# A SiLU MLP's first product: three of eight feature pairs by 11 block products instead of 12, in five half chunks

## The chip, the core and the metric

The kernel runs on one core of one Trainium2 chip. The core has a matrix engine (PE, with its weight loads shown as PEld), a vector engine (DVE), a scalar engine (ACT), a general engine (POOL), a queue that issues transfers (SP) and 16 DMA engines. Each engine executes its own instructions in the order in which the program issued them; they meet at semaphores. The metric is device time in microseconds.

## What is computed

A delta-rule recurrence over 768 tokens of 4 batches and 8 heads, then an MLP with SiLU. The MLP is what the change is about: `x` is 3072 x 384, `w_in` 384 x 2048, `w_out` 2048 x 384.

```python
def _attn_ref(q, k, v, beta):            # B, H, S, D = 4, 8, 768, 48
    k_n = k / (np.linalg.norm(k, axis=-1, keepdims=True) + 1e-06)
    for t in range(S):
        y[:, :, t] = np.einsum('bhd,bhde->bhe', q[:, :, t], state)
        v_old = np.einsum('bhde,bhd->bhe', state, kt)
        state = state + bt[:, :, :, None] * np.einsum('bhd,bhe->bhde', kt, vt - v_old)

def _moe_ref(x, w_in, w_out):
    h = x @ w_in
    g = h * (1.0 / (1.0 + np.exp(-h)))
    return (g @ w_out).astype(np.float32)
```

The weights come as 64-bit floats and are narrowed to f32 on the chip; all products are f32.

## The kernel before

The sequence is cut into six chunks of 128 tokens, each chunk into two halves of 64. For a half chunk, `solve(c)` advances the recurrence and leaves `xTs[c, hf]`: the MLP's input, transposed, as three blocks of 128 input features by 256 columns (4 batches x 64 tokens). `hidden(c, hf)` (line 1022) makes the first product and its SiLU; `combine(c, hf)` (line 1122) makes the second product in a Strassen form on 192-column matmuls (line 1136; chunk 0 has a plain second product, `project`). `feed_forward` is one after the other.

`hidden` runs over eight feature pairs `f`. A pair is two blocks of 128 output features, each the sum of three matmuls (128x128 weights from `w_in`, 256 columns from `xTs`), so six matmul calls that fill one PSUM bank of 512 columns; one ACT instruction then writes SiLU of all 512 columns to a `gT` tile (line 1039). An f32 matmul call is two instructions in the trace. The banks of room `M`, `m0` and `m1`, alternate from pair to pair (`bank`, line 61). Three pairs share a `gT` tile; there are three such tiles, the last with one slot of 512 columns unused. Every second or third pair DVE adds the sums that `combine` needs (`sum_g`, line 1110).

The order of the work is the order of the program text: `pin` (line 78) ties every instruction to the one before it on its engine. The stages are Python generators; `go` and `run` advance them by a step, and a `yield` is where other work can come in between. In the main loop (lines 1499 to 1527) the nine steps of `solve(c)`, then `prepare(c + 1)` (scores of the next chunk) and `invert(c + 1)` (31 rank-one updates on DVE) are interleaved with the steps of the MLP. `hidden(c, 0)` for chunks 2 to 5 falls beside the end of `solve(c)`, where ACT makes two bursts of seven copies (`even_heads`, line 915: six to `xT` and one to `part`), and beside `prepare(c + 1)`: DVE transposes from `stage` (`turn_blocks`, line 471), scores (`score`, line 504) that ACT copies out and DVE masks (`mask`, line 526; `by_act` and `by_dve`, lines 531 and 534). `hidden(c, 1)` falls beside `invert`. The last half, chunk 5's second, runs with nothing beside it.

The keys of chunk `c` lie in `kbufs[c % 2]`, in rows of 64 of which 48 are used; `square` (line 361), `turn` (line 481) and `update` (line 841) read them. `stage` holds chunk 1's turned keys and queries, and from chunk 2 on, in its first three quarters, the blocks that `load_blocks` brings in (line 149).

Of the kernel before, what the change touches and what calls it, by code (L numbers as in the profile page):

```python
# [10 lines left out]
FP32 = mybir.dt.float32  # L11
U32 = mybir.dt.uint32
ACTF = mybir.ActivationFunctionType
ALU = mybir.AluOpType
# [5 lines left out]
def kernel(  # L20
# [10 lines left out]
    nc = tc.nc  # L31
    B, H, S, D = q.shape
    DM, DFF = moe_w_in.shape
    P = 128
    C = P
    assert S % C == 0 and D == 48 and H == 8 and B == 4 and DM == H * D and DM == 3 * P
    NCH = S // C
    NP = H // 2
    BH = B * H
    W = 64  # L40
    T = 32
    NB = C // T
    NKT = DM // P
    NFF = DFF // P
    HB = B // 2
    HH = HB * H
    GT = B * W
    FG = 3
# [7 lines left out]
    mlp = ctx.enter_context(tc.tile_pool(name="mlp", bufs=2))  # L56
    banks = ctx.enter_context(tc.tile_pool(name="banks", bufs=1, space=PSUM))
    A, CC, M = deque(("a0", "a1", "a2")), deque(("c0", "c1", "c2")), deque(("m0", "m1"))
    kept_banks = {tag: banks.tile([P, 512], FP32, name=f"pb_{tag}", tag=tag) for tag in CC}

    def bank(room, name):

        tag = room[0]
        room.rotate(-1)
        return kept_banks.get(tag) or banks.tile([P, 512], FP32, name=name, tag=tag)
# [3 lines left out]
    def behind(later, earlier, how=NoSync):  # L69

        tc.add_manual_dep(
            later.ins, earlier.ins.name,
            mybir.DependencyInfo(how, mybir.DependencyReason.DATA), reason="order",
        )
# [3 lines left out]
    def pin(op):  # L78

        engine = op.ins.engine  # L80
        if engine in pins:
            behind(op, pins[engine])
        pins[engine] = op
        return op
# [3 lines left out]
    def in_line(dma):  # L88

        if line:  # L90
            behind(dma, line[-1])
        if pace:
            behind(dma, pace.pop(), Sync)
        line.append(dma)
        return dma
# [8 lines left out]
    def go(steps, n=1):  # L104
        for _ in range(n):
            next(steps, None)
# [9 lines left out]

    kbufs = [const.tile([P, B, NP, 2, W], FP32, name=f"kb{s}") for s in range(2)]
    zbuf = const.tile([P, B, 2, NP, W], FP32, name="z")
    vfs = {}
    LO, HI = slice(0, W), slice(W, P)  # L120
    HALVES = (LO, HI)

    def on(e, hf, g):

        return HALVES[hf ^ e ^ g]

    sums_of_g = const.tile([P, 2, NFF // 2, C], FP32, name="sums_of_g")
# [5 lines left out]
    def load_pair(to, src, c, bs):  # L133

        for g in range(bs.start // HB, bs.stop // HB):
            us = slice(HB * g, HB * (g + 1))
            for e, hf in ((g, None), (1 - g, 0), (1 - g, 1)):
                rows = slice(0, P) if hf is None else on(e, hf, g)
                tokens = slice(c * C, (c + 1) * C) if hf is None else slice(c * C + hf * W, c * C + (hf + 1) * W)
                in_line(nc.sync.dma_start(  # L140
                    out=to[rows, us, :, e, 0:D],
                    in_=src[us, e::2, tokens, :].rearrange("b h t d -> t b h d"),
                ))

    RUN = C // T * D
    stage = const.tile([P, B * NP * 2 * C], FP32, name="stage")
# [16 lines left out]
    def in_blocks(c):  # L163

        return 1 < c < NCH
# [7 lines left out]

    def load_k(c, bs=ALL):
        if c < NCH:
            load_pair(kbufs[c % 2], k, c, bs)

    def load_q(c, bs=ALL):
        if c < NCH:
# [25 lines left out]
    for e in range(2):  # L205
        for g in range(2):
            to, of = slice(HH * e + HH // 2 * g, HH * e + HH // 2 * (g + 1)), slice(HH // 2 * g, HH // 2 * (g + 1))
# [6 lines left out]
    w_in = const.tile([P, NKT, DFF], FP32, name="w_in")  # L214
# [83 lines left out]
    def narrow_w_out(i):  # L298
# [14 lines left out]
        out=above[0:W], in_=above[0:W], pattern=[[1, W]], compare_op=ALU.is_gt, fill=0.0,  # L313
# [3 lines left out]
        out=above[W:P], in_=above[W:P], pattern=[[1, W]], compare_op=ALU.is_gt, fill=0.0,  # L317
# [5 lines left out]
    for j in range(NB):  # L323
        rows = slice(T * j, T * (j + 1))
# [36 lines left out]
    def square(c, b):  # L361

        if b == 0:
            sums[c] = small.tile([P, BH], FP32, name="ss", bufs=1)[:]
        if c > 2:
            squared[c, b] = zbuf[:, b].rearrange("p s a w -> p (s a) w")[:, :, 0:D]
        elif b % HB == 0:
            tag = "g" if c > 0 or b > 0 else "x"
            both = work.tile([P, HB, H, D], FP32, name="sq", tag=tag, bufs=1)
            for u in range(HB):  # L370
                squared[c, b + u] = both[:, u]
        kb = kbufs[c % 2][:, b].rearrange("p a e w -> p (a e) w")[:, :, 0:D]
        pin(nc.gpsimd.tensor_tensor(out=squared[c, b], in0=kb, in1=kb, op=ALU.mult))

    def add_squares(c, b):
# [155 lines left out]
    def by_act(to, of):  # L531
        return pin(nc.scalar.copy(to, of))  # L532
# [219 lines left out]
    xTs, parts = {}, {}  # L752
# [88 lines left out]
    def update(c, g, hf):  # L841

        if c == NCH - 1 and hf == 1:
            return
        pu = bank(CC, "pu")
        for u, p, e, n, of, _ in of_heads():
            rows = on(e, hf, g)
            yield pin(nc.tensor.matmul(  # L848
                pu[of, n * D : (n + 1) * D], lhsT=kbufs[c % 2][rows, g * HB + u, p, e, 0:D],
                rhs=zbuf[rows, g * HB + u, hf, p, 0:D], start=True, stop=True,  # L850
            ))
        to = states[g][:, :, :, 0:D]
        pin(nc.vector.tensor_tensor(out=to, in0=to, in1=by_heads(pu), op=ALU.add))
# [160 lines left out]
    gTs = {}  # L1014

    def hidden_of(c, hf, f):

        if (c, hf) == (0, 1):
            return turned_kq[:].rearrange("p b j a t -> p (b j a t)")[:, f * 2 * GT : (f + 1) * 2 * GT]
        return gTs[f // FG][:, f % FG, :]  # L1020

    def hidden(c, hf):

        for f in range(NFF // 2):
            assert ("in", f) in narrowed
            ph = bank(M, "phid")
            for j in range(2):
                for a in range(NKT):
                    pin(nc.tensor.matmul(  # L1029
                        ph[:, j * GT : (j + 1) * GT],  # L1030
                        lhsT=w_in[:, a, (2 * f + j) * P : (2 * f + j + 1) * P],
                        rhs=xTs[c, hf][:, a, :],
                        start=(a == 0), stop=(a == NKT - 1),
                    ))
                if j == 0:
                    yield
            if f % FG == 0 and (c, hf) != (0, 1):
                gTs[f // FG] = mlp.tile([P, FG, 2 * GT], FP32, name="gT", bufs=3)
            pin(nc.scalar.activation(  # L1039
                out=hidden_of(c, hf, f), in_=ph[:], func=ACTF.Silu, scale=-0.5 if in_blocks(c) else 0.5  # L1040
            ))
            if c > 0 and f % FG == 1 and f >= FG:
                for which in (S1, S2):
                    sum_g(which, f // FG - 1)
            yield
# [41 lines left out]
    def sum_w():  # L1087
# [14 lines left out]
    S1, S2, S3, S4 = (  # L1102
        (0, (0, 1), (1, 1), ALU.add), (1, 0, (0, 0), ALU.subtract),
        (0, (0, 0), (0, 1), ALU.subtract), (1, (1, 0), 1, ALU.subtract),
    )
# [4 lines left out]
    def sum_g(which, g):  # L1110
        k, left, right, op = which
        fs = group(g)
        of = [
            sums_of_g[:, x, fs] if isinstance(x, int) else
            gTs[g][:, 0 : fs.stop - fs.start, x[0] * GT + x[1] * C : x[0] * GT + (x[1] + 1) * C]
            for x in (left, right)
        ]
        pin(nc.vector.tensor_tensor(out=sums_of_g[:, k, fs], in0=of[0], in1=of[1], op=op))  # L1118
# [154 lines left out]
    for b in range(B):  # L1273
        square(0, b)
# [95 lines left out]
    def run(n=1):  # L1370

        for _ in range(n):
            name = next(needed, None)
            if name is not None:
                until(name)
            go(pieces)
            begin_soon()
# [121 lines left out]
    for c in range(1, NCH):  # L1499
        if c > 1:  # L1500
            solving = solve(c)
            for n in range(9):
                go(solving)
                run((2, 2, 2, 2, 1, 1, 2, 2, 2)[n])
                if n == 5:
                    pieces = chained(pieces, feed_forward(c, 0), feed_forward(c, 1))
        assert next(solving, 0) == 0
        go(long_2, 99)
        if c + 1 < NCH:
            ready = prepare(c + 1)  # L1510
            go(ready)
            run(2)
            step = block_steps(c + 1)
            for _ in ready:
                run(2)
            run(6)
            for n, _ in enumerate(invert(c + 1, step)):
                run(int(n % 4 != 3 and n != 24))
                if n == 3:
                    load_k(c + 2)  # L1520
                    if in_blocks(c + 2):
                        load_blocks(k, c + 2, ALL)
            after = lengths(c + 2) if c + 2 < NCH else iter(())
            for _ in range(8 if c == 1 else 10):
                run()
                go(after, 4)
            go(after, 99)
# [31 lines left out]
```

## Time and profile before

| what | value |
|---|---|
| runs | 653.5, 654.77, 656.47 us, median 654.77 |
| profiled execution | 652.37 us, its span 650.4 us |
| granted TensorE clock, mean | 0.99 |
| feature pairs in all | 12 half chunks x 8 |
| L1029, matmuls of `hidden` | 1152 instructions, 260.1 us busy |
| L1039, SiLU of a pair | 0.597 us each |
| `hidden` of the last half | 608.13 to 628.85 us |

The profile is of one execution. PE, PEld, DVE, ACT and POOL are given as busy time, share of the span and number of instructions. A row of a group has the line, engine, operation, output and inputs, the shape and the count; then busy us in all, mean ns of one; then the engine's idle time just before them and what ended most of it. A row of the timeline has the start in us, the length in us, the engine, the line, the operation and, in brackets, the idle time before it and what released it. The chain of waits is followed back from the last instruction, at each step to what released it or to the instruction before it on its engine. Matmul records overlap, since the engine is pipelined: a record of 0.379 us can be followed by the next after 0.216.

### The profile page before, as it was taken

The page shows a single profiled execution, that of the slowest core. Times are in us where ns is not written, and L with a number is a line of the kernel's source. Part 1 is how long each engine was busy: PE and PEld are TensorE (multiplying, and loading weights), DVE is VectorE, ACT ScalarE, POOL GpSimd, SP SyncE. Part 2 cuts the span into 40 slices and gives each one's busy share as a digit, 9 for nine tenths or more (in the row PEclk, how much of TensorE's full clock was granted, in tenths as well). Part 3 has the DMA queues.
Part 4 walks back from the last instruction along what each step waited for, and adds up shares of the span by engine and source line. Part 5 has one row for each costly group of instructions (what it writes and reads, how often), then busy time and mean ns, then how long its engine had stood idle before and what let it go on. Part 6 is the DMA issues. An engine that isn't in the chain of part 4 may idle for free.

```text
span 650.4 us, 21395 instructions
## 1 busy us (share of the span) xinstructions
PE 627.6 (96%) x9416; PEld 548.0 (84%) x9416; DVE 397.6 (61%) x911; ACT 213.8 (33%) x497; POOL 90.9 (14%) x92
## 2 busy tenths in 40 slices
PE   7878899999989999999999999999999999999997
PEld 5577778756779989989989989989989989889997
DVE  5875689997764987453986453987454974103112
ACT  2455663332342122451122452122451122451111
POOL 5023631334101020010020010020011000000000
PEclk9979999999989999999999999999999999999999
DMA  9876534250288324268324268324173024100101
GB/s 136 209 165 206 192 75 104 98 97 3 53 154 148 58 73 60 50 136 143 59 76 57 48 131 146 61 74 60 28 153 72 10 65 60 40 13 1 25 0 25
DMA packets 145676, 54.70 MB, mean 84 GB/s; under 512 B 117152, under 2 KB 138912, under 8 KB 145584
## 3 DMA queue, kind: packets, MB, share of 16 engines
q1 hardware_dynamic: 143136, 52.93, 39.6%
q8 instruction: 74, 1.21, 0.8%
q10 hardware_dynamic: 2448, 0.41, 0.4%
q14 instruction: 18, 0.15, 0.1%
HBM read 40.14 MB, written 11.01 MB: 79 GB/s over the span
## 4 chain that ended last, share of the span: by engine, by line
PE 91%; DMA 2%; issue 2%; DVE 2%; ACT 1%; SPq 1%; DVEq 0%
PE phid L1029 38%; PE px L1136 16%; PE py L1136 12%; PE po L1064 5%; PE pb_c L828 3%; PE pa L517 2%; PE pb_c L816 2%; PE pyc L907 2%; PE pb_c L1064 2%; PE pb_c L848 1%; PE pb_c L336 1%; PE pyc L894 1%; DMA kb<-in_k_dram 1%; PE pt L488 1%; PE py L770 1%
## 5 line engine op out<-in xcount | busy, mean ns | idle before, releaser
L1029 PE MATMUL phid<-xT,w_in 128*128 128x256 f32 x1152 | 260.1, 383 | 2.1 <-DMA xT<-part 2.0
L1029 PEld LDWEIGHTS phid<-xT,w_in 128*128 128x128 f32 x1152 | 216.9, 191 | 34.4 <-issue 3.0
L1039 ACT ACTIVATE gT<-phid 128x512 f32<-128x512 f32 x88 | 52.5, 597 | 149.8 <-PE phid L1029 145.2
L615 DVE SCALAR_TENSOR_TENSOR rank<-g,step,x 128x31 f32<-128x31 f32 (+15 forms) x124 | 49.8, 401 | 35.8 <-DMA g<-blocks 32.3
L1118 DVE TENSOR_TENSOR sums_of_g<-gT 128x384 f32<-128x384 f32 (+1 forms) x60 | 29.9, 518 | 59.0 <-ACT gT L1039 48.4
L1136 PE MATMUL py<-w_out,sums_of_g 128*128 128x192 f32 x320 | 56.8, 329 | 0.0
L1136 PE MATMUL px<-sums_of_w,sums_of_g 128*128 128x192 f32 x320 | 56.8, 329 | 0.0
L1136 PEld LDWEIGHTS px<-sums_of_w,sums_of_g 128*128 128x128 f32 x320 | 52.2, 190 | 0.5
L1136 PEld LDWEIGHTS py<-w_out,sums_of_g 128*128 128x128 f32 x320 | 52.2, 190 | 0.4
L620 DVE TENSOR_TENSOR x<-x,rank 128x31 f32<-128x31 f32 (+15 forms) x124 | 42.5, 343 | 4.3
L455 POOL TENSOR_TENSOR vf<-vf,n_slot 128x768 f32<-128x768 f32 x10 | 15.0, 1516 | 169.3 <-DMA vf<-in_v_dram 125.3
L476 DVE STREAM_TRANSPOSE kq<-stage 128x512 f32<-128x512 f32 x28 | 28.5, 1114 | 12.0 <-DMA stage<-in_q_dram 10.4
L532 ACT COPY xT<-pyc 48x128 f32<-48x128 f32 (+2 forms) x126 | 32.6, 259 | 1.6
L1136 PE MATMUL px<-sums_of_w,gT 128*128 128x192 f32 x160 | 28.4, 329 | 0.0
L1136 PE MATMUL py<-w_out,gT 128*128 128x192 f32 x160 | 28.4, 329 | 0.0
L1136 PE MATMUL px<-w_out,gT 128*128 128x192 f32 x160 | 28.0, 327 | 0.0
L1136 PEld LDWEIGHTS px<-w_out,gT 128*128 128x128 f32 x160 | 26.4, 190 | 0.5
L538 POOL COPY g<-x 64x256 f32<-64x256 f32 x4 | 5.0, 1241 | 154.5 <-DVE x L623 154.5
L1136 PEld LDWEIGHTS py<-w_out,gT 128*128 128x128 f32 x160 | 26.1, 190 | 0.3
L1136 PEld LDWEIGHTS px<-sums_of_w,gT 128*128 128x128 f32 x160 | 26.1, 190 | 0.2
L828 PEld LDWEIGHTS pb_c<-vf,xi 64*64 64x64 f32 x736 | 23.5, 138 | 3.2 <-issue 2.9
L1147 DVE TENSOR_TENSOR o<-o,kept 128x192 f32<-128x192 f32 (+1 forms) x29 | 11.5, 422 | 24.0 <-ACT kept L1144 24.0
(221 smaller groups left out, 921.6 us busy)
## 6 DMA issues: line engine op xcount, KB each, us to landing
vf<-in_v_dram SPq DMA_DIRECT2D x48, 96.0 KB, 3.2
out_dram<-o SPq DMA_DIRECT2D x42, 96.0 KB, 2.2
w_out<-in_moe_w_in_dram SPq DMA_DIRECT2D x4, 768.0 KB, 4.4
sums_of_w<-in_moe_w_out_dram SPq DMA_DIRECT2D x4, 768.0 KB, 5.9
blocks<-ap SPq DMA_DIRECT2D x44, 64.0 KB, 1.9
g<-blocks SPq DMA_DIRECT2D x5, 512.0 KB, 3.5
kb<-in_k_dram SPq DMA_DIRECT2D x12, 192.0 KB, 5.1
kb<-in_k_dram SPq DMA_DIRECT2D x24, 96.0 KB, 4.6
```

The costliest lines, as they stand in the source:

```text
L455: pin(nc.gpsimd.tensor_tensor(out=vf, in0=vf, in1=of, op=ALU.mult))
L476: pin(nc.vector.transpose(out=kqs[c, b][:, :, j, :].rearrange("p a (i m) -> p a m i", i=T), in_=src.rearrange("p a (m d) -> p a m d", d=D) ...
L517: pin(nc.tensor.matmul(pa[e][half, p * n * W : (p + 1) * n * W], lhsT=kq[rows, p, 0, half], rhs=kq[rows, p, js[0] : js[-1] + 1, half], sta ...
L532: return pin(nc.scalar.copy(to, of))
L615: pin(nc.vector.scalar_tensor_tensor(out=tv, in0=g[:, 0:m, m : m + 1].to_broadcast([P, m, n]), scalar=step[:, m : m + 1], in1=x[:, m : m + ...
L620: yield pin(nc.vector.tensor_tensor(out=x[:, 0:m, m:T], in0=x[:, 0:m, m:T], in1=tv, op=ALU.add))
L828: yield pin(nc.tensor.matmul(pz[rows, n * D : (n + 1) * D], lhsT=xis[g][rows, u * H + 2 * p + e, :], rhs=vfs[c][rows, hf, g * HB + u, p, : ...
L1029: pin(nc.tensor.matmul(ph[:, j * GT : (j + 1) * GT], lhsT=w_in[:, a, (2 * f + j) * P : (2 * f + j + 1) * P], rhs=xTs[c, hf][:, a, :], star ...
L1039: pin(nc.scalar.activation(out=hidden_of(c, hf, f), in_=ph[:], func=ACTF.Silu, scale=-0.5 if in_blocks(c) else 0.5))
L1064: pin(nc.tensor.matmul(pos[i][:, 0:DM], lhsT=hidden_of(0, hf, f // 2)[:, at : at + C], rhs=w_outs[f // HFF][:, f % HFF, :], start=(f == 0) ...
L1118: pin(nc.vector.tensor_tensor(out=sums_of_g[:, k, fs], in0=of[0], in1=of[1], op=op))
L1136: pin(nc.tensor.matmul(to, lhsT=at, rhs=quarter(f, *b) if isinstance(b, tuple) else sums_of_w[b][:, f], start=start and f == 0, stop=f == ...
```

## The change

With `x(a, t)` the 128 x 128 block of input block `a` and column half `t`, and `w(a, j)` the weight block from input block `a` to output block `j` of a pair, a pair is 12 products of 128x128 weights with 128 columns: two column halves, two output blocks, three input blocks. For pairs 1, 3 and 5 the change computes the eight of input blocks 0 and 1 by seven products and sums (Winograd's form), and keeps the four of input block 2: 11 matmul calls of 128 columns in place of six of 256.

- The sums of weights (`w1` to `w4`) are made once by five DVE instructions in chunk 2, after step 3 of `solve(2)`. They are kept in the unused last quarter of `stage` and in a part of `kbufs[1]` that comes free: from chunk 3 on the keys of odd chunks are stored there without the 16 unused columns a row (`keys_of`).
- The sums of inputs (`x1` to `x5`) are made once in a half by four DVE instructions, after the third matmul of pair 0. They lie in the unused slot of the third `gT` tile and in a slot of `sums_of_g`.
- `hidden_by_seven` takes the place of `hidden` in the first halves of chunks 2 to 5 and in the last half. A product goes in five steps: s1 with four matmul calls to blocks `d` and `b` of its bank, then an ACT copy of both; s2 with one call to `a` and two to `d`, then a DVE addition of `a` to the copied part and an ACT copy of `d`; s3 and s4 with one call to `a` each, and each with a DVE addition; s5 with two calls to `a`, then two SiLU instructions. The steps alternate with the six calls of the next pair, made as before, p1 to p6. The bank of the product is thus held from s1 to the first SiLU of s5.
- The stage has 16 yields, as before.

```diff
+    KEPT = B * H * D
+
+    def keys_of(c):
+
+        if c % 2 == 0 or c == 1:
+            return kbufs[c % 2]
+        flat = kbufs[1][:].rearrange("p b a e w -> p (b a e w)")
+        return flat[:, 0:KEPT].rearrange("p (b a e d) -> p b a e d", b=B, a=NP, e=2)
...
-            load_pair(kbufs[c % 2], k, c, bs)
+            load_pair(keys_of(c), k, c, bs)
...
-        kb = kbufs[c % 2][:, b].rearrange("p a e w -> p (a e) w")[:, :, 0:D]
+        kb = keys_of(c)[:, b].rearrange("p a e w -> p (a e) w")[:, :, 0:D]
...
-                pu[of, n * D : (n + 1) * D], lhsT=kbufs[c % 2][rows, g * HB + u, p, e, 0:D],
+                pu[of, n * D : (n + 1) * D], lhsT=keys_of(c)[rows, g * HB + u, p, e, 0:D],
...
+    by_seven = (1, 3, 5)
+    NS = len(by_seven)
+    tail = stage[:, B * NP * RUN :]
+    key_tail = kbufs[1][:].rearrange("p b a e w -> p (b a e w)")[:, KEPT:]
...
+    w1, w2, w3 = blocks_of(tail, 0), blocks_of(key_tail, 0), blocks_of(tail, NS)
+    w4s = [blocks_of(tail, 2 * NS, 2), blocks_of(key_tail, NS, 1)]
...
+    def sums_of_blocks():
...
+        a11, a12, a21, a22 = (of(a, j, 0, NS) for j, a in ((0, 0), (0, 1), (1, 0), (1, 1)))
+        pin(nc.vector.scalar_tensor_tensor(
+            out=w1, in0=a21, scalar=-1.0, in1=a22, op0=ALU.mult, op1=ALU.subtract
+        ))
+        pin(nc.vector.scalar_tensor_tensor(
+            out=w2, in0=w1, scalar=-1.0, in1=a11, op0=ALU.mult, op1=ALU.subtract
+        ))
+        pin(nc.vector.tensor_tensor(out=w3, in0=a11, in1=a21, op=ALU.subtract))
+        at = 0
+        for to in w4s:
+            n = to.shape[1]
+            pin(nc.vector.tensor_tensor(
+                out=to, in0=of(1, 0, at, n), in1=w2[:, at : at + n], op=ALU.subtract
+            ))
+            at += n
...
+    def hidden_by_seven(c, hf):
+
+        xT = xTs[c, hf]
+        scale = -0.5
+        for g in (2, 0, 1):
+            gTs[g] = mlp.tile([P, FG, 2 * GT], FP32, name="gT", bufs=3)
+        free = gTs[2][:, FG - 1, :]
+        x1, x5 = free[:, 0:C], free[:, C : 2 * C]
+        x2, x3, x4 = free[:, 2 * C : 3 * C], free[:, 3 * C : 4 * C], sums_of_g[:, 0, NFF // 2 - 1]
...
+        def plain(f):
+
+            ph = bank(M, "phid")
+            for j in range(2):
+                for a in range(NKT):
+                    w = w_in[:, a, (2 * f + j) * P : (2 * f + j + 1) * P]
+                    mm(ph[:, j * GT : (j + 1) * GT], w, xT[:, a, :], a == 0, a == NKT - 1)
+                    yield
+            silu(hidden_of(c, hf, f), ph[:])
+
+        def product_steps(f):
+
+            i = by_seven.index(f)
+            ph, to = bank(M, "phid"), hidden_of(c, hf, f)
+            a, b, d = ph[:, 0:C], ph[:, C : 2 * C], ph[:, 2 * C : 3 * C]
+            at_11, at_22, at_21 = to[:, C : 2 * C], to[:, 2 * C : 3 * C], to[:, 3 * C : 4 * C]
+            mm(d, w3[:, i], x3, start=True)
+            mm(d, w_block(i, 2, 1), x(2, 1))
+            mm(b, w_block(i, 1, 0), x(1, 0))
+            mm(b, w_block(i, 2, 0), x(2, 0), stop=True)
+            by_act(to[:, C : 3 * C], ph[:, C : 3 * C])
+            yield
+            mm(a, w_block(i, 0, 0), x(0, 0))
+            mm(d, w_block(i, 1, 1), x4)
+            mm(d, w_block(i, 2, 1), x5, stop=True)
+            add_x(at_11, a, at_11, ALU.add)
+            by_act(at_21, d)
+            yield
+            mm(a, w2[:, i], x2)
+            add_x(at_21, a, at_21, ALU.add)
+            yield
+            mm(a, w1[:, i], x1)
+            add_x(at_22, a, at_22, ALU.add)
+            yield
+            mm(a, w4(i), x(1, 1))
+            mm(a, w_block(i, 2, 0), x(2, 1), stop=True)
+            silu(to[:, 0:C], a)
+            silu(to[:, C:], to[:, C:])
+            yield
+
+        differ = free[:, 0 : 2 * C].rearrange("p (n t) -> p n t", t=C)
+        first = plain(0)
+        go(first, 3)
+        add_x(differ, xT[:, 0::2, C : 2 * C], xT[:, 0::2, 0:C], ALU.subtract)
+        add_x(x3, x(1, 1), x(0, 1), ALU.subtract)
+        add_x(x2, x(1, 1), x1, ALU.add)
+        add_x(x4, x(1, 0), x2, ALU.subtract)
+        yield
+        go(first, 99)
+        yield
+        for n, f in enumerate(by_seven):
+            by, beside = product_steps(f), plain(f + 1)
+            go(by)
+            go(beside)
+            yield
+            go(by)
+            go(beside)
+            yield
+            go(beside)
+            go(by)
+            go(beside)
+            go(by)
+            yield
+            go(beside)
+            go(by)
+            go(beside, 99)
+            if n == 1:
+                for which in (S1, S2):
+                    sum_g(which, 0)
+            yield
+        last = plain(NFF // 2 - 1)
+        go(last, 3)
+        yield
+        go(last, 99)
+        for which in (S1, S2):
+            sum_g(which, 1)
+        yield
+
     def hidden(c, hf):
 
+        if in_blocks(c) and (hf == 0 or c == NCH - 1):
+            yield from hidden_by_seven(c, hf)
+            return
...
                 go(solving)
+                if c == 2 and n == 3:
+                    sums_of_blocks()
                 run((2, 2, 2, 2, 1, 1, 2, 2, 2)[n])
```

## The prediction

> **What bounds the kernel now.** First the page's shares, then the chain of waits.
>
> ```profile
> span 650.4 us, 21395 instructions
> PE 627.6 (96%) x9416; PEld 548.0 (84%) x9416; DVE 397.6 (61%) x911; ACT 213.8 (33%) x497; POOL 90.9 (14%) x92
> ...
> PE 91%; DMA 2%; issue 2%; DVE 2%; ACT 1%; SPq 1%; DVEq 0%
> ```
>
> PE is busy 96% of the span and is 91% of the chain, so a microsecond that PE saves or loses reaches the end. The chain in order of time (start, length, what) shows the stage that is changed: `hidden` of chunk 4's first half, and of the last half, where nothing else runs.
>
> ```profile
> 473.95 5.38 PE phid L1029 x24
> 481.38 2.79 PE phid L1029 x12
> 486.07 10.56 PE phid L1029 x48
> ...
> 608.13 20.72 PE phid L1029 x96
> 628.85 5.20 PE px L1136 x32
> ```
>
> 96 instructions in 20.72 us are 215.8 ns for one of 256 columns. An f32 matmul is two instructions, so a plain matmul call (p) is 0.432 us and a feature pair, six calls, 2.59 us. PE has no idle time here: over 608.13 to 628.85 and over 469.35 to 496.63 its busy time equals the window.
>
> **The price of a block product.** The trace has no f32 matmul of 128 columns with 128x128 weights. Two neighbours bound it.
>
> ```profile
> 183.06 0.60 PE L488 MATMUL pb_c<-ident,kb 128*128 128x128 f32 x4
> ...
> 479.16 0.30 PE L433 MATMUL pg<-pick,spread 128*128 128x32 f32 x2
> ...
> L433 PE MATMUL pg<-pick,spread x12: 192/276/297, 19.9 to 479.2; 128*128 128x32 f32 x12
> ```
>
> Four transposes of 128 columns span 0.60 us and one lasts 0.272: (0.60 - 0.272)/3 = 0.109 us from one to the next. This is the lower end, set by the columns. In L433 32 columns are 0.027 us of streaming; the first instruction of the pair lasts 0.192 and the pair spans 0.30, so the second ends 0.11 after the first (0.112 in the unrounded records): it stands waiting for its weights. That is the price of a 128x128 weight load by itself, the upper end. I take 0.110, so a block product call (q) is 0.220 us. Farther off, the 192-column rows of L1136 step at 2.60/16 = 0.1625 us, but their columns alone need that.
>
> The Trainium skill, "TensorE: Matmul & The Clock Gate", section "Back-to-back issue gap", speaks against the change: in a stream of load and matmul pairs 128 columns cost about 81 ns, against about 56 for the matmul alone. Scaled to the 0.109, that estimate is 0.159 us; L433 speaks against it, and no long stream of this shape is in the trace.
>
> **PE's work.** A changed pair has 11 calls of 0.220 = 2.42 us for 2.59: -0.17 us. Three pairs in five halves, 15 pairs: -2.6 us (-2.85 at 0.109, -1.9 at 0.112).
>
> **The new waits.** Block `a` of the PSUM bank is a running sum: DVE must read it before PE may add to it again, three times in a product. Prices, from the groups by shape:
>
> ```profile
> L532 ACT COPY ap<-pa 128x256 f32<-128x256 f32 x22 | 8.1, 372 | 14.1 <-PE pb_c L517 12.9 <-DVE ap L535 1.2
> L664 DVE TENSOR_TENSOR rank<-sums_of_w 128x128 f32<-128x128 f32 x1 | 0.3, 293 | 0.0
> L1136 PE MATMUL py<-w_out,gT 128*128 128x192 f32 x160 | 28.4, 329 | 0.0
> ```
>
> An ACT copy of 256 columns takes 0.372; one of 128 0.26 (L532 xT rows); silu of 128 about 0.27, of 384 0.49 (L1160). A DVE addition of 128 columns takes 0.29. A 128-column matmul lasts 0.273 (192 columns 0.326, 256 0.379). In the last half phid ends at 628.85 and its silu starts at 628.89: ACT follows by 0.04; DVE by 0.05 (L821). PE's next load follows DVE by 0.05 (L500 ends at 7.61, the load starts at 7.66), and an exposed load costs 0.11. So after a group's last matmul slot, ACT can start 0.20 later, DVE 0.21; PE can stream 0.16 after the reader ends.
>
> Now one pair walked with nothing else on PE, from the start of its product's first step (s1 to s5 the product's steps, p1 to p6 the plain pair's calls):
>
> ```
> s1 4 calls 0.00-0.88   ACT copies 256 columns 1.08-1.45
> p1         0.88-1.31
> s2 a       1.31-1.53   d waits for the copy: 1.61-2.05 (0.08 lost)
>                        DVE adds a 1.74-2.03; ACT copies d 2.25-2.51
> p2 p3      2.05-2.91
> s3         2.91-3.13   DVE adds 3.34-3.63
> p4         3.13-3.56
> s4         3.79-4.01   (0.23 lost)  DVE adds 4.22-4.51
> p5         4.01-4.44
> s5         4.67-5.11   (0.23 lost)  silu of a 5.31-5.58, of the rest to 6.07
> p6         5.11-5.54
> next bank  5.74        (0.20 lost): it is this product's, free after silu of a
> ```
>
> The pair takes 5.74 us; work is 5.01, waits 0.73. Before, two pairs took 5.18. Three pairs in each of five halves: 15 x 0.73 = 11.0. Scoring or state updates of the next chunk lie inside some waits (a bank wait and the copy wait in chunk 2, s5's and the copy's in 3, a bank wait in 4, the copy's in 5): -0.8. **Standing waits: +10.2.**
>
> **Queues in the first halves.** There ACT and DVE, both in order, already hold other work. ACT around chunk 4's hidden:
>
> ```profile
> 474.06 0.58 ACT L532 COPY part<-pyc 48x512 f32<-48x512 f32 x1 [1.29 <-DMA stage<-in_q_dram]
> 474.65 1.61 ACT L532 COPY xT<-pyc 48x128 f32<-48x128 f32 x6
> 476.77 0.60 ACT L1039 ACTIVATE gT<-phid 128x512 f32<-128x512 f32 x1 [0.51 <-PE phid L1029]
> 477.27 0.56 ACT L532 COPY part<-pyc 48x512 f32<-48x512 f32 x1
> 477.86 1.61 ACT L532 COPY xT<-pyc 48x128 f32<-48x128 f32 x6
> ...
> 475.75 2.05 DVE L476 STREAM_TRANSPOSE kq<-stage 128x512 f32<-128x512 f32 x2 [1.67 <-DMA stage<-in_q_dram]
> 481.40 0.42 DVE L527 TENSOR_TENSOR ap<-pa,above 128x256 f32<-128x256 f32 x1
> ```
>
> Two bursts of seven copies (2.2 us) come from `even_heads`; today they only make a silu late, which the second bank hides. In chunk 4 s1 and p1 begin at 473.95; PE wants the copy by 475.48, but it stands behind the first burst (to 476.17) and PE goes on at 476.70: 1.2 lost. That makes the first addition late, then the two transposes of L476 (2.05) stand ahead of the second: +0.5; after the second scoring four masks (L527) stand ahead of one: +0.35. Likewise chunk 2, where the copy follows the second burst (to 284.75) and PE wants it at 283.36: +1.9; chunk 3: copy +0.5, then the copy of d behind the second burst +0.6; chunk 5: silu of a behind the second burst, +0.5. **Together +5.6.** Were each burst through in time, 0.
>
> **Costed at nothing.** The four x sums, 1.3 us of DVE per half: in chunk 4 between 471.4 and 472.7, with plain pair 0 (2.59 us of PE) as cover; uncovered 1.3 each. The five weight sums once in chunk 2, 2.4 us of DVE (L1118 rows: 0.55 for 384 columns): in a stretch where DVE sat idle 5.28 us ahead of L853 at 265.03; uncovered at most 2.4. The keys' denser tile: the same DMAs with the same 192-byte pieces, the same queues, the same loads. The two silus for one add 0.2 us to ACT, which is 33% busy, and lie in the walk.
>
> **Sum.** -2.6 + 10.2 + 5.6 = +13.2 us. The profiled execution is 652.37 us (span 650.4, the rest around it), so 665.6; the median of the three runs shown is 654.77, 2.4 above it. I forecast **668.0** (own range 663 to 672). A measurement of this kernel can tell about 0.5%, 3.3 us.
>
> **Rivals.**
> - *No queueing* (0.15): ACT's bursts and DVE's masks land so that the late PE meets free engines: -2.6 + 10.2 = +7.6, **662.4**. For it: each stall moves PE away from the burst. Against: the bursts are released by PE's own L907 just ahead.
> - *The waits are covered* (0.09), the other side: at s4 and s5 one plain call, 0.432 us, lies between PE's `a` and its next; if the round trip (0.21 + 0.29 + 0.16 = 0.66) fell under that, only PE's work changes: -2.6, **652.2**, or 657.8 with the bursts, no change by the bound. It decides from 0.43 us on. For it: matmul ends in the records are modelled. Against: the silu's 0.04 behind that end is measured on ACT. Even so PE's best is -2.85, under 3.3.
> - *The weight loads bind* (0.07): at the row of 0.1625 a call pair is 22 x 0.1625 = 3.58 us, +0.99 each, +14.8; waits shrink by about 0.05 each, to some 13 in all: +28, **682**. For it: PEld is 84% busy; against it L433. By the page's 0.159 it would be +13.6 in place of +14.8.
> - *One bank, two users* (0.07): s2's `a` also waits for the copy, as it lies in the same bank: 0.22 more a pair, +3.3, **671.3**. Before, ACT read one bank while PE wrote the other. "Advanced Engine Details and Errata", section "Bank Collisions", of the Trainium skill says the three engines can't use a bank in the same cycle; by it PE's writes and the 0.29 us addition under s2's d calls would share, at most 15 x 0.29 = 4.4 us. No run here shows such sharing yet.
>
> The forecast has 0.62. 658 to 675 leaves out the covered case and the weight loads, 0.16 in all, and the tails. Faster 0.03 (only something unseen gives over 2.85), same 0.09, slower 0.88.
>
> **What would show it.** Right: block matmuls 0.110 us apart; PE idle of about 0.23 us ahead of s4 and s5, released by DVE's addition; of 0.2 us at the bank change, released by ACT; over a microsecond at s2 in chunks 2 and 4, released by ACT's copy; the last half's hidden about 1.7 us longer than 20.72. Wrong: steps of 0.16, or a last half shorter than 20.7 us, or first halves where PE never waits on ACT.

## The result and the profile after

The changed kernel takes **676.2 us** (median of 6 runs, 672.35 to 677.11), the kernel before 654.13 (6 runs, 651.95 to 660.95): ratio **1.0314** with the interval 1.0262 to 1.0366. It is slower by three per cent. The profiled execution took 676.64 us with a span of 674.7, 24.3 more than the span of 650.4 before; the prediction had +13.2. The two medians are 22.1 apart; what follows is taken from the two profiled executions.

The shares of the page of the changed kernel (busy time, then the chain by engine):

```profile
span 674.7 us, 21820 instructions
PE 644.6 (96%) x9566; PEld 548.6 (81%) x9566; DVE 416.8 (62%) x981; ACT 223.7 (33%) x542; POOL 90.7 (13%) x92
...
PE 77%; DVE 7%; DMA 6%; ACT 4%; SPq 2%; issue 2%; POOL 0%; DVEq 0%; POOLq 0%; ACTq 0%
```

PE is still busy 96% of a longer span, which could be read as "PE has more work". PE's part of the chain fell from 91% to 77%, which would say the reverse; but the chain of e7 below also has 77%, at a span of 653.3, so neither share tells the loss. The last half's `hidden`, where nothing else runs, in the chain of waits (start, length, what):

```profile
629.58 10.05 PE phid L1090 x56
...
639.65 6.10 PE phid L1090 x34
...
645.77 7.36 PE phid L1090 x36
653.14 5.20 PE px L1290 x32
```

It lasts from 629.58 to 653.14, 23.56 us, for 20.72 before. The chain calls all but 0.04 us of it PE, and the list of PE's waits in the whole kernel shows little (total us, times, longest):

```profile
PE phid L1090 <- ACT gT L541: 4.6, 5, 1.8
...
PE phid L1090 <- DMA xT<-part: 2.3, 3, 0.9
PE phid L1090 <- DVE gT L1087: 1.3, 3, 0.9
PE phid L1090 <- ACT gT L1093: 0.6, 1, 0.6
```

These are 6.5 us without the DMA, which was there before, while the five halves grew by 23. A block matmul's record is 0.27 us long though the next may start 0.11 later, so a wait below some 0.2 us leaves no gap between records. Such waits are read from starts alone. So I took the stage's length, from the first `phid` matmul of a half to its first `px` matmul, in every kernel that was run (us):

| kernel | chunk 2 | chunk 3 | chunk 4 | chunk 5 | last half |
|---|---|---|---|---|---|
| before | 25.18 | 27.08 | 27.18 | 26.08 | 20.72 |
| after | 31.34 | 30.69 | 32.45 | 31.23 | 23.56 |
| e1, last half alone | 25.17 | 27.08 | 27.18 | 26.09 | 23.56 |
| e2, no readers | 26.00 | 29.30 | 27.95 | 28.50 | 22.22 |
| e3, plain pairs in 128 columns | 25.89 | 27.79 | 28.24 | 26.78 | 21.44 |
| e4, sums alone | 25.18 | 27.08 | 27.18 | 26.09 | 20.72 |
| e5, own bank for b and d | | | | | 22.68 |
| e6, middle pair plain | 27.06 | 28.88 | 29.16 | 30.88 | 23.56 |
| e7, own banks and more cover | | | | | 20.54 |
| e8, PE kept busy | 29.81 | 30.66 | 32.45 | 29.72 | 23.56 |

After against before: +6.16, +3.61, +5.27, +5.15 and +2.84, together **+23.03** of the 24.3. The other 1.3 lie ahead of the `hidden` of chunk 2 (0.7) and of chunk 5 (0.6). They can be chance: over all profiled executions, chunk 2's `hidden` starts anywhere from 275.1 to 283.9 us, and the stretch between chunk 4's last `hidden` and chunk 5's first takes 27.9 to 29.5.

### The profile page after: what moved, and what is told of

It is laid out like the page before. It is cut to its first block, busy times and chain, and to the rows that moved or that the text cites. A ratio compares the mean times of both kernels' runs of the same rounds, so it can differ in the third digit from the quotient of the medians.

```text
span 674.7 us, 21820 instructions
## 1 busy us (share of the span) xinstructions
PE 644.6 (96%) x9566; PEld 548.6 (81%) x9566; DVE 416.8 (62%) x981; ACT 223.7 (33%) x542; POOL 90.7 (13%) x92
## 4 chain that ended last, share of the span: by engine, by line
PE 77%; DVE 7%; DMA 6%; ACT 4%; SPq 2%; issue 2%; POOL 0%; DVEq 0%; POOLq 0%; ACTq 0%
PE phid L1183 17%; PE phid L1090 15%; PE px L1290 13%; PE py L1290 9%; PE po L1218 5%; PE pa L526 2%; PE pb_c L837 2%; ACT xT L541 2%; DMA stage<-in_q_dram 2%; DVE rank L624 2%; DVE x L629 2%; PE pb_c L1218 2%; SPq L896 1%; PE pyc L916 1%; PE pb_c L825 1%
## 5 line engine op out<-in xcount | busy, mean ns | idle before, releaser
L1183 PE MATMUL phid<-xT,w_in 128*128 128x256 f32 x672 | 152.1, 384 | 0.5 <-DMA xT<-part 0.4
L1183 PEld LDWEIGHTS phid<-xT,w_in 128*128 128x128 f32 x672 | 126.7, 191 | 18.7 <-DMA xT<-part 0.8
L1090 PE MATMUL phid<-xT,w_in 128*128 128x256 f32 (+1 forms) x450 | 102.4, 353 | 6.1 <-ACT gT L541 3.0
L1090 PEld LDWEIGHTS phid<-xT,w_in 128*128 128x128 f32 x450 | 68.6, 191 | 17.9 <-ACT gT L541 8.0
L1193 ACT ACTIVATE gT<-phid 128x512 f32<-128x512 f32 x48 | 28.7, 597 | 87.8 <-PE phid L1183 77.5
L1087 DVE TENSOR_TENSOR gT<-phid,gT 128x128 f32<-128x128 f32 x45 | 13.1, 290 | 65.6 <-PE phid L1090 65.6
L1093 ACT ACTIVATE gT<-phid 128x512 f32<-128x512 f32 (+1 forms) x40 | 19.0, 474 | 48.8 <-PE phid L1090 48.8
L837 PEld LDWEIGHTS pb_c<-vf,xi 64*64 64x64 f32 x736 | 25.0, 146 | 3.2 <-issue 2.6
```

Of the source, the lines that this page charges most:

```text
L837: yield pin(nc.tensor.matmul(pz[rows, n * D : (n + 1) * D], lhsT=xis[g][rows, u * H + 2 * p + e, :], rhs=vfs[c][rows, hf, g * HB + u, p, : ...
L1090: pin(nc.tensor.matmul(to, lhsT=left, rhs=right, start=start, stop=stop, skip_group_check=True))
L1093: pin(nc.scalar.activation(out=to, in_=of, func=ACTF.Silu, scale=scale))
L1183: pin(nc.tensor.matmul(ph[:, j * GT : (j + 1) * GT], lhsT=w_in[:, a, (2 * f + j) * P : (2 * f + j + 1) * P], rhs=xTs[c, hf][:, a, :], star ...
L1193: pin(nc.scalar.activation(out=hidden_of(c, hf, f), in_=ph[:], func=ACTF.Silu, scale=-0.5 if in_blocks(c) else 0.5))
```

## The experiments

My theory was the prediction's: the loss is the standing waits of the block products, with the queues of ACT and DVE on top in the first halves. The rivals were the weight loads, one bank with two users, and the extra work that was costed at nothing. Edits are against the changed kernel.

**e1: the new form in the last half alone**, where no scoring or state update runs beside it.

```
-        if in_blocks(c) and (hf == 0 or c == NCH - 1):
+        if c == NCH - 1 and hf == 1:
             yield from hidden_by_seven(c, hf)
```

> The block products in the last half alone; the four first halves are made the old way; weight sums and denser keys stay. Theory of the waits (DVE and ACT must read a bank before PE may go on in it): hidden of the last half stays at some 23.6 us against 20.72 before, and that is all: +2.8 us over before, ratio about 1.004. Theory of the queues and the clock: the other 21 us of the changed kernel belong to the first halves, where ACT and DVE have other work and PE's idle time halves its clock, so the mean granted clock goes back to 0.99. Rival, that the weight sums or the denser keys cost: more than +4 us.

Measured: 659.85 us, ratio 1.0096 (1.0058 to 1.0134); profiled span 652.2. The last half is 23.56 us, to the hundredth that of the changed kernel, and all other halves are those of before. The chain of waits:

```profile
607.06 16.17 PE phid L1090 x90
...
623.26 7.36 PE phid L1090 x36
630.62 5.20 PE px L1290 x32
```

So the standing cost of three pairs is +2.84, where the prediction's walk gave 3 x (0.73 - 0.17) = 1.7: it is too low by 0.38 a pair. The timed ratio was more than the 1.0044 that 2.84 us make; e9 comes back to it.

**e2: PE's instructions without their readers.** The copies and the additions between the steps are left out, so the three pairs' hidden values are not formed; PE's calls and the two SiLUs stay.

```
-            by_act(to[:, C : 3 * C], ph[:, C : 3 * C])
...
-            add_x(at_11, a, at_11, ALU.add)
-            by_act(at_21, d)
...
-            add_x(at_21, a, at_21, ALU.add)
...
-            add_x(at_22, a, at_22, ALU.add)
...
-            silu(to[:, 0:C], a)
-            silu(to[:, C:], to[:, C:])
+            silu(to[:, 0 : 3 * C], ph[:, 0 : 3 * C])
+            silu(to[:, 3 * C :], a)
```

> All five halves with the 11 block calls, but without the two ACT copies and three DVE additions of each product: it leaves out the combination of the partial sums, so blocks of the output are not the reference's; two SiLU instructions read the bank at the end. Theory of the waits: PE's work alone is left, 15 pairs x (22 x 0.1118 - 12 x 0.2158) = -2.0 us, the last half at about 20.3 us, ratio about 0.997. Rival, that the shape itself is slow (weight loads of 128 columns at 0.16 a step): last half over 23 us, +14 us in all.

Measured: 662.12 us, ratio 1.0142 (1.0088 to 1.0197), the last half 22.22. The expectation fell, and the list of PE's waits of this kernel shows why:

```profile
PE phid L1090 <- ACT gT L1093: 5.8, 14, 1.3
```

PE waits 14 times for the SiLUs. They now read all of the product's bank, and one plain call lies between them and the next use of that bank. The edit took five readers away and made the last ones longer, so it did not measure PE's work by itself. What holds of it: without the round trips in the middle, the five halves cost +7.7 us over before instead of +23.0.

**e3: the shape alone.** All eight pairs of the five halves are made plain, but each matmul of 256 columns is split into two of 128: twice the weight loads, the same streaming, no block products. The sums of weights and inputs are left out, the denser keys stay.

```
+        n_cols = C if in_blocks(c) and (hf == 0 or c == NCH - 1) and SPLIT else GT
...
+                    for at in range(0, GT, n_cols):
+                            ph[:, j * GT + at : j * GT + at + n_cols],
...
+                            rhs=xTs[c, hf][:, a, at : at + n_cols],
```

`SPLIT` is true.

> No block products: in the five halves every plain pair is made by 12 calls of 128 columns in place of six of 256, the same result. It measures the shape with no reader between. At 0.1118 a step a pair is 24 x 0.1118 = 2.68 us for 2.59: 40 pairs, +3.7 us, the last half 21.5 us. By the Trainium skill's 81 ns for 56 (TensorE: Matmul & The Clock Gate, Back-to-back issue gap), scaled to 0.159 a step: +49 us.

Measured: 656.45 us, ratio 1.0052 (1.0006 to 1.0098), span 654.4. The last half in its chain of waits:

```profile
611.37 21.44 PE phid L1183 x192
```

192 instructions in 21.44 us are **0.1117 us each**, within 2% of the 0.110 of the prediction and at its upper end, about the step of L433, which streams 32 columns on weights of the same size. The five halves together grew by 3.9 us, 0.6%, as the ratio has it. The rival of 0.1625 is refuted: it would have made this half 31.2 us. The Trainium skill, "TensorE: Matmul & The Clock Gate", section "Back-to-back issue gap", has load and matmul pairs of 128 columns take 81 ns where the matmul alone takes 56; scaled to this kernel, the prediction made 0.159 of it. Here 128 columns cost 3.5% over half of a 256-column step (0.1117 against 0.1079), so that penalty does not carry over to this f32 stream.

**e4: the extra work without the products.** All pairs plain, but with the four x sums in the five halves, the weight sums in chunk 2 and the denser keys (the sums are made and not used).

```
-        if in_blocks(c) and (hf == 0 or c == NCH - 1):
-            yield from hidden_by_seven(c, hf)
-            return
+        extra = in_blocks(c) and (hf == 0 or c == NCH - 1)
...
+                    if f == 0 and extra:
+                        inputs_of_blocks(c, hf)
```

> Weight sums, input sums and denser keys as in the change, but every pair made the old way from 256 columns, so the sums are made and not used. Theory: they are hidden, 0 within 0.5%. Rival, that they hold up DVE ahead of the transposes and the transfers: up to 1.3 us in each of five halves and 2.4 us once, +8.9 us.

Measured: 651.82 us, ratio 0.999 (0.9971 to 1.0009). Every half is as long as before within 0.01 us, the last one too:

```profile
607.46 20.72 PE phid L1201 x96
```

The work that was costed at nothing costs nothing by itself. No matmul reads the sums here, so a wait of the products for them is not in this run; in chunk 2 and in the last half of the changed kernel the first block matmul (at 282.57 and 632.00) follows pair 0's last one by its step of 0.216, so plain pair 0 covers the sums, as the prediction named.

**e5: blocks b and d in a bank of their own**, in the last half alone (with e1's condition). The waits on `a` itself stay.

```
-            a, b, d = ph[:, 0:C], ph[:, C : 2 * C], ph[:, 2 * C : 3 * C]
+            pd = bank(A, "phid")
+            a, b, d = ph[:, 0:C], pd[:, C : 2 * C], pd[:, 2 * C : 3 * C]
...
-            by_act(to[:, C : 3 * C], ph[:, C : 3 * C])
+            by_act(to[:, C : 3 * C], pd[:, C : 3 * C])
...
-            mm(a, w_block(i, 0, 0), x(0, 0))
+            mm(a, w_block(i, 0, 0), x(0, 0), start=True)
```

> Block products in the last half alone, with blocks b and d of a product in a PSUM bank of their own, so that a's bank is touched by DVE alone until the SiLU. The order of the calls is unchanged. Theory, that any two accesses of one bank are put in order (a's matmul behind ACT's copy of d, ACT's second copy behind DVE's addition, s3 behind that copy): the waits fall from 1.08 to 0.73 us a pair, the last half from 23.6 to about 22.5 us. Rival, that only the round trips of the running sum count: 23.6 as it was.

Measured: one run, 659.55 us; the last half is 22.68 (from 613.05 to 635.73):

```profile
613.05 6.21 PE phid L1090 x36
...
630.92 4.81 PE phid L1090 x22
635.73 5.20 PE px L1291 x32
```

One shared bank therefore costs (23.56 - 22.68)/3 = **0.29 us a pair**. What is left of the waits is (22.68 - 20.72 + 0.39)/3 = 0.78 a pair, where 0.39 is PE's work saved in three pairs. The walk's 0.73 is near the price of this layout in sum, though the wait for a SiLU's bank here falls on p1 and not on the next s1. The timelines of the last half of the changed kernel (start, length, engine, line, what) show the sharing. PE:

```profile
638.03 0.49 PE L1090 MATMUL phid<-gT,stage 128*128 128x128 f32 x2
638.35 1.78 PE L1090 MATMUL phid<-xT,w_in 128*128 128x128 f32 x10
639.97 0.39 PE L1090 MATMUL phid<-sums_of_g,w_in 128*128 128x128 f32 x2
...
640.42 1.03 PE L1090 MATMUL phid<-xT,w_in 128*128 128x256 f32 x4
641.33 0.49 PE L1090 MATMUL phid<-gT,kb 128*128 128x128 f32 x2
...
642.20 0.49 PE L1090 MATMUL phid<-gT,stage 128*128 128x128 f32 x2
...
643.08 0.49 PE L1090 MATMUL phid<-xT,stage 128*128 128x128 f32 x2
...
644.15 0.49 PE L1090 MATMUL phid<-gT,stage 128*128 128x128 f32 x2
```

ACT beside it (in brackets how long the engine sat idle, and what released it):

```profile
639.22 0.37 ACT L541 COPY gT<-phid 128x256 f32<-128x256 f32 x1 [0.35 <-PE phid L1090]
641.02 0.27 ACT L541 COPY gT<-phid 128x128 f32<-128x128 f32 x1 [1.42 <-DVE gT L1087]
```

and DVE:

```profile
640.69 0.29 DVE L1087 TENSOR_TENSOR gT<-phid,gT 128x128 f32<-128x128 f32 x1 [3.79 <-PE phid L1090]
641.86 0.29 DVE L1087 TENSOR_TENSOR gT<-phid,gT 128x128 f32<-128x128 f32 x1 [0.88 <-PE phid L1090]
642.73 0.29 DVE L1087 TENSOR_TENSOR gT<-phid,gT 128x128 f32<-128x128 f32 x1 [0.58 <-PE phid L1090]
```

One pair goes from 638.03 to 644.15, 6.12 us for the 5.74 of the walk. A pair of block instructions that spans 0.49 instead of 0.39 stands behind a wait with its load exposed: s3, s4, s5 and the next s1 all do. Three orders come from the bank alone. The group from 638.35 holds `a` of s2, which starts in the unrounded records at 639.65, behind the end of ACT's copy at 639.60, though that copy reads b and d. DVE's first addition reads `a` and starts at 640.69, behind the d calls, not after `a`. And ACT's copy of d is released by DVE's addition, although both only read; s3 at 641.33 stands behind that copy (end 641.28). In e5 the same copy starts without DVE, 0.04 us behind the end of PE's last d call:

```profile
617.78 0.27 ACT L541 COPY gT<-phid 128x128 f32<-128x128 f32 x1 [0.84 <-PE phid L1090]
```

and `a` of s2 starts at 616.91 in the unrounded records, while the first copy still runs (to 616.94).

**e6: the middle pair plain in the first halves**, which drops pair 1's products in chunks 2 to 5.

```
+            if f == 1 and hf == 0:
+                for g in (1, 2):
+                    beside = plain(g)
+                    go(beside, 3)
+                    yield
+                    go(beside, 99)
+                    yield
+                continue
```

> As the changed kernel, but pair 1 of the four first halves is made the old way, so that no product meets the two bursts of seven ACT copies; pairs 3 and 5 stay. Theory of the queues: a first half then costs two undisturbed pairs, 2 x 0.95 = 1.9 us, and the clock has no idle time there to fall: 4 x 1.9 + 2.8 = +10.4 us over before, ratio 1.016. Rival, that all pairs cost alike: two thirds of the first halves' 20.8 us and the last half, +16.7 us, ratio 1.026.

Measured: 666.44 us, ratio 1.0123 (1.0039 to 1.0208), span 660.9. Chunks 2, 3 and 4 are 1.88, 1.80 and 1.98 above before: two products without a queue in their way, at 0.95 each. Chunk 5 is 4.80 above; it has 6.8 us at half clock from 568.0, worth up to 3.4, behind waits for `xT` that are there in every version. By that the five halves come to +13.3 for the +10.4 expected; the rival's ratio of 1.026 lies outside the measured interval. What pair 1 loses more than its own 0.95 is the queues: after less e6 less 0.95, in chunk 2 also less 1.5 of clock (e8), is 1.8, 0.9 and 2.3 in chunks 2 to 4. In chunk 5, where e6 is disturbed, three products at 0.95 and 1.5 of clock leave 0.8 of the 5.15. Together **5.8**. In the timeline of chunk 2 of the changed kernel the burst can be seen ahead of the copy:

```profile
283.26 0.57 ACT L541 COPY part<-pyc 48x512 f32<-48x512 f32 x1
283.85 1.62 ACT L541 COPY xT<-pyc 48x128 f32<-48x128 f32 x6
285.49 0.37 ACT L541 COPY gT<-phid 128x256 f32<-128x256 f32 x1
...
285.92 0.58 PE L1090 MATMUL phid<-xT,w_in 128*128 128x128 f32 x2 [1.80 <-ACT gT L541]
```

**e7: own banks and more cover**, in the last half alone: e5 with the product in a third bank, and two plain calls (0.86 us) for one ahead of s4 and of s5, which comes behind p6.

```
-            ph, to = bank(M, "phid"), hidden_of(c, hf, f)
+            ph, to = bank(CC, "phid"), hidden_of(c, hf, f)
...
-            go(beside)
             go(by)
-            go(beside)
+            go(beside, 2)
             go(by)
             yield
-            go(beside)
-            go(by)
             go(beside, 99)
+            go(by)
```

> As the kernel with own banks, last half alone, but with both banks of a product out of the plain pairs' room (three of each to go round) and two plain calls in place of one between s3 and s4, s4 and s5. Theory of the round trip (0.66 us against a plain call of 0.43): with 0.86 us of cover the waits at s4, s5 and the bank go, the last half takes 20.72 - 3 x 0.13 = 20.3 to 20.6 us, under the 20.72 of before. Rival, that the partial sums cost by themselves (bank shared by two engines at a time, more instructions): over 21.5 us.

Measured: one run, 655.21 us; the last half is 20.54. In its PE timeline the calls follow without an exposed load (0.39 for the pair of block instructions, not 0.49):

```profile
615.98 1.03 PE L1090 MATMUL phid<-xT,w_in 128*128 128x256 f32 x4
616.84 0.39 PE L1090 MATMUL pb_c<-gT,stage 128*128 128x128 f32 x2
```

With the waits gone the products gain 0.18 us in a half, of the 0.39 that PE's work allows.

**e8: PE kept busy in the long waits.** Dummy matmuls ahead of s2 of chunk 2's first product and ahead of the first calls in chunk 5.

```
+            if c == 2 and n == 0:
+                busy(3)
...
-        go(first, 3)
+        for _ in range(3):
+            if c == NCH - 1 and hf == 0:
+                busy(1)
+            go(first)
```

> The changed kernel with idle matmuls put where PE waits longest: three 384-column calls ahead of s2 of chunk 2's first product, one ahead of each of the first three matmuls of chunk 5's hidden, 1.9 us of PE each, into banks that nobody reads. Theory of the clock: the two stretches of 3.41 us at half clock that follow these waits (0.54 and 0.61 in chunk 5) are gone, the mean clock is 0.99 and not 0.982, and the kernel is up to 3.4 us faster than the changed one, ratio to before 1.026. Rival, that the clock falls for other reasons or costs nothing: same time, or up to 1.9 us more.

Measured: 672.36 us, ratio 1.0244 (1.0147 to 1.034), an interval that overlaps that of the changed kernel; span 668.8. The profile is clearer: chunk 2 is 1.53 shorter than after, chunk 5 1.51, chunks 3 and 4 equal. Busy time by stretch in the changed kernel, chunk 2:

```profile
core 0: us, PE busy (x) PEld busy (x) DVE busy (x) ACT busy (x) POOL busy (x), PEclk, DMA share, GB/s
284.00:286.00 2.00, 0.20 (x2) 0.08 (x1) 0.00 (x0) 1.78 (x7) 0.00 (x0) 1.00 0.86 154
286.00:288.00 2.00, 2.00 (x8) 1.83 (x9) 0.52 (x2) 0.21 (x1) 1.18 (x1) 0.55 0.74 159
288.00:290.00 2.00, 2.00 (x39) 1.93 (x41) 1.82 (x2) 0.24 (x2) 1.73 (x2) 0.60 0.67 155
290.00:292.00 2.00, 2.00 (x42) 1.60 (x34) 1.35 (x4) 1.29 (x4) 0.00 (x0) 1.00 0.21 50
```

and in e8, around the same wait:

```profile
281.00:283.00 2.00, 2.00 (x8) 1.01 (x6) 0.00 (x0) 1.90 (x7) 0.00 (x0) 1.00 0.75 143
283.00:285.00 2.00, 2.00 (x31) 1.87 (x34) 0.91 (x2) 0.37 (x2) 0.00 (x0) 1.00 0.80 147
```

PE idle for 1.80 us is followed by a stretch at half clock, from 286.18 and 3.41 us long; with the wait filled the clock stays at 1.00. The stretch in chunk 5, from 583.14, comes behind three waits for `xT` (0.94, 0.54 and 0.77 us), which the kernel before has too, so the 1.51 there is not the price of a wait that the products added.

**e9: e1's kernel again**, in more rounds and on another chip, for its open ratio, and **e10: e7's kernel** beside it.

> The changed form in the last half alone, timed once more in more rounds. Its profile showed +2.84 us in that half and every other half as before. If the waits in the last half are all that it adds, the ratio is 1.0044, within 1.003 to 1.006. If something outside that half is longer in the runs that were not profiled (the larger tile of sums, the denser keys, which this kernel keeps), it is about 1.0096 as first timed, 1.007 or more.

> The last half alone with own banks and two plain calls of cover, timed. If the last half is all that differs, its 0.18 us gain is nothing that can be told: ratio 0.9997, within 0.997 to 1.003. If the last-half kernel has a cost elsewhere, it is here too: 1.004 or more.

Measured: e9 657.92 us, ratio 1.0032 (1.0001 to 1.0064), with the last half at 23.57; e10 656.94, ratio 1.002 (0.9982 to 1.0057), the last half 20.54 again. The 1.0044 of e1's profile lies inside e9's interval, and 1.0096 does not: no steady cost outside the last half was seen again. In the first session the three runs of e1 (of 10) with a granted clock of 0.989 or more average 654.1 us and the 12 such runs of before (of 25) 652.0, 2.1 apart, so the excess goes with a lower granted clock in e1's other seven; why it had so many of them stays open. e10 can't be told from before.

## Why the prediction came out as it did

The direction, the place and the mechanism were right in the main, the price of the waits was too low, and 676.2 lies just above the range of 658 to 675. Against its own execution the sum was 11.1 us short (24.3 for 13.2). Term by term:

| term | predicted | measured | from |
|---|---|---|---|
| PE's work | -2.6 | -1.95 | step of 0.1118 (0.1117 in e3): 15 x (22 x 0.1118 - 12 x 0.2158) |
| standing waits | +10.2 | +16.2 | last half: (2.84 + 0.39)/3 = 1.08 a pair, 15 pairs |
| queues | +5.6 | +5.8 | remainder, after against e6 |
| clock | none | +3.0 | e8, chunks 2 and 5 |
| sums, keys | 0 | 0 | e4 |
| outside the five halves | none | +1.3 | lengths; can be chance |

The first four make 23.05, for 23.03 in the five halves; as the queues are what the others leave, that sum is no proof by itself. The check is in e6: the 1.08 of the last half, less 0.13 of PE's work saved, is 0.95 a product, 1.90 for two, and chunks 2 to 4 measure 1.88, 1.80 and 1.98.

- **The bound and the block product.** Right: PE sets the end, and the step is 0.112 for 0.110, the upper of the two bounds. It takes 0.65 us off the gain.
- **The standing waits** are the mis-sized term, +16.2 for +10.2. The walk let PE write `a` while ACT copies b and d, and let DVE and ACT read one bank side by side. e5 shows 0.78 a pair when these can, close to the walk's 0.73, and 0.29 more when all share one bank. This is the rival "one bank, two users": its place at s2 was right, its price of 0.22 was not, as it saw only the first of the three orders. By the traces it is the program's order of accesses to one bank, each named as a releaser; for a loss by accesses in the same cycle there is neither sign nor need. That 15 x 0.29 = 4.4 us is also the prediction's figure for such a loss is chance: there 0.29 is the length of an addition. Every bank is one tile (one named buffer) of the program, so the runs don't tell whether the order hangs on the bank or on the tile. The 0.8 that was taken off for covered waits was not seen in pairs 3 and 5: in e6 they cost in chunks 2 to 4 what they cost in the last half; for pair 1 it can't be told from the queues. So of the 6.0 that the term was short, 4.4 are the shared bank, 0.8 the walk (0.78 for 0.73) and 0.8 the cover.
- **The queues** were right: +5.8 for +5.6, chunk by chunk 1.8, 0.9, 2.3, 0.8 for 1.9, 1.1, 2.05, 0.5, as what the other terms leave; chunk 5's figure rests on the 0.95 of the other chunks. ACT's burst ahead of the copy is where it was put, with PE idle 1.80 us in chunk 2 and 1.25 in chunk 4.
- **Costed at nothing** was right (e4).
- **The clock** was missing. The prediction made a microsecond of idle PE cost a microsecond. In the profiled execution the wait of 1.8 us in chunk 2 cost 1.5 more; chunk 5's 1.5 came behind waits that the kernel before has without such a loss, so it belongs to this execution.
- **The rivals.** "No queueing" and "the weight loads bind" fall by e6 and e3. "The waits are covered" has its point of decision right: with two plain calls for one, 0.86 us for the round trip of 0.66, and banks of their own, the loss goes (e7). What is then left for the change is at most 1.95 us in all five halves, 0.3%, below what a measurement can tell.

So one multiplication less in twelve, in 15 of the kernel's 96 pairs, is worth 15 x 2.59/12 = 3.2 us at most. The step of 128 columns, longer than half of one of 256, leaves 1.95 of it, 0.3%, and the order that the change puts between three engines costs eight times that.

## What to carry to other kernels

Before multiplications are saved by running sums in PSUM, count the round trips: each needs other PE work as long as matmul to reader to matmul (0.66 us here) behind it, and in a program that orders its accesses as this one does, the readers of different blocks need different banks, even when they only read. Measure a stage by its length from first to first instruction, as waits below a matmul record's length leave no gap in any list of waits. And reckon with a slow clock behind a long wait of PE, which may or may not come.

## What the runs showed of the hardware that was not expected

- **The clock can drop after a short idle time.** PE busy 0.20 of the 2.00 us from 284.00 was followed by 3.41 us at half clock (0.55 and 0.60 in the means of the next two stretches), and filling the wait made that half 1.53 us shorter. The Trainium skill, "TensorE: Matmul & The Clock Gate", section "Part 1: The HAM clock gate", has the clock halve after at least one idle window of about 3.4 us and come back after as long a busy one. The second agrees with the 3.41; the first does not with 1.80, and here the measured number stands. It does not follow every wait either: chunk 4 has waits of 1.25 and 0.92 us and none behind them, and the waits for `xT` ahead of chunk 5 had none in the kernel before, 3.4 us of it here and 6.8 in e6. In every profile the half-clock stretches begin whole multiples of 3.413 us apart: 64 and 87 of them between those from 67.73, 286.18 and 583.14 here, 44 between those from 39.64 and 189.83 in the kernel before. So a stretch does not begin where a wait ends, and where a wait falls in this raster may decide as well as its length. PE was busy 1.61 and 1.84 of the 3.41 us just ahead of the two stretches here, but no limit comes out: 1.83 in e7 (from 66.31) was followed by none, 2.33 in e2 (from 249.06) by one. From which idle time on it happens was not tried.
- **An f32 step of 128 columns** takes 0.1117 us beside 0.2158 for 256 (e3), and a load that stands exposed behind a wait adds 0.10 to the pair of instructions (0.49 for 0.39).
